# The transpose of a pair's softmax factors: one unit later, and in the bank of the products with V

## The chip, the cores and the metric

One core of a Trainium2 chip. The metric is the device time of one execution in microseconds (us), median over runs. Engines are named as in the profile: PE is TensorE, PEld its weight loads, DVE is VectorE, ACT ScalarE, POOL GpSimd, and SP the SyncE queue that issues all DMAs.

## The reference, cut to what matters

Block-causal attention over 8 batches, 8 heads, 576 positions and 64 columns per head, then a gated convolution layer, then a Fourier mixing layer with a feed-forward net:

```python
scores = scale * np.matmul(q, k.transpose(0, 1, 3, 2))
scores = np.where(mask, scores, -1000000000.0)          # 64-wide blocks, block_i >= block_j
scores = scores - np.max(scores, axis=-1, keepdims=True)
attn = np.exp(scores)
attn = attn / (np.sum(attn, axis=-1, keepdims=True) + 1e-09)
attn_out = np.matmul(attn, v)
...
x = (sigmoid(causal_conv(x)) * (x @ w_val)) @ w_out
u = x + np.real(np.fft.fft(np.fft.fft(x, axis=1), axis=2))
out = u + np.maximum(norm(u) @ w_ch1, 0.0) @ w_ch2
```

What the change touches is the division by the row sums. The kernel multiplies the products with V by the reciprocals of the sums; these are the "softmax factors" of a pair.

## The kernel before, in words

The kernel has two phases. Phase 1 does the attention, the gated layer and the Fourier mixing; phase 2 does the normalization and the feed-forward net, and is not touched by the change.

Phase 1 works on pairs of heads: 32 pairs, four to a batch. A pair has nine units. Units 0 to 7 are a tile of 128 query rows of one of the two heads (two heads by four tiles); unit 8 is the last 64 rows of both. The loop at the end of `phase1` steps through all units n; in each step it writes the scores of unit n (tile `sc`, line 406 and 407, or 165 to 167 for unit 8), takes the row maxima (`mx`, line 438) and the exponentials (`PB`, line 451) of units just before, and transposes the exponentials of unit n - 6 (`pt`, line 506; ACT copies them out, line 512). Between them come pieces of the dense work of the batch before (`psv`, `psx`, `psy`, `pss`).

At the step that is ten units behind, `emit_recip` makes the reciprocals `re` of a pair's row sums on DVE (lines 458 to 465). One step later `emit_factors` transposes them on PE (`rt`, line 474) into a PSUM bank of the pool `ps_pt`, whose two banks also take all transposes `pt` and the last piece `ave` of the products with V. ACT copies the ten rows out (line 479), SP writes them to DRAM (`f_d`, line 480) and reads them back three times (line 483), spread over 64 partitions each, into the tile `XF`, since there they are factors along the free axis. After the ninth unit `emit_av` makes the products with V (`av`, line 535, the single bank of the pool `ps_av`; `ave`, a bank of `ps_pt`). `scaled_x` multiplies them by the factors into `XF` on DVE (lines 549 and 548). From `XF` follow the cast `XH` and the first tap `gate` on ACT (lines 57 and 63), the rest `XL` on POOL and four taps on DVE (line 564).

The scores have three banks (`ps_sc`) in turn. A pair fills eight of them: one each for units 0 and 1, and 2 and 3, one each for units 4 to 7, and two for unit 8. So the first scores of a pair take the bank that unit 7 of the pair before held, and can only be written when its exponentials are done.

The order of the instructions on an engine is not simply that of the code: a scheduler places each instruction by the order of the code and by its own idea of when its inputs are ready. Within an engine the order is then fixed.

`tq` holds the chains of work that wait for a bank of `ps_pt` to be emptied; a `Chain` runs its stages one per step. `load` fetches q and k of a pair two ahead (`qraw`, `kraw`, lines 323 and 325). `spread` writes the queries of the next pair into the tiles `QQ` (lines 377 and 379), `split` into `QD` (line 353); all of these are DMAs of SP too.

Of the kernel before, what the change touches and what calls it, by code (L numbers as in the profile page):

```python
# [8 lines left out]
F32 = mybir.dt.float32  # L9
# [8 lines left out]
def kernel(  # L18
# [14 lines left out]
    B, NP, P, S = q.shape  # L33
    D = 512
# [67 lines left out]
    def phase1():  # L102
        with ExitStack() as c1:
# [6 lines left out]
            ps_pt = c1.enter_context(tc.tile_pool(name="ps_pt", bufs=2, space=bass.MemoryType.PSUM))  # L110
            ps_sc = c1.enter_context(tc.tile_pool(name="ps_sc", bufs=3, space=bass.MemoryType.PSUM))
            ps_av = c1.enter_context(tc.tile_pool(name="ps_av", bufs=1, space=bass.MemoryType.PSUM))
# [71 lines left out]
            def tick(chains):  # L184
                for c in chains:
                    if c.at < len(c.stages):
                        c.run(c.at + 1)
                    if c.at == len(c.stages) and c in live:
                        live.remove(c)
# [128 lines left out]
            def load(p):  # L318
                if p >= NPAIR:
                    return  # L320
                b, hp = divmod(p, NP)
                qraw[p] = raw_p.tile([P, S], F32, tag="raw", name="qraw")
                nc.sync.dma_start(out=qraw[p], in_=q[b, hp])
                kraw[p] = raw_p.tile([P, S], F32, tag="raw", name="kraw")
                nc.sync.dma_start(out=kraw[p], in_=k[b, hp])

            def load_v(p):
                if p >= NPAIR:
                    return
                b, hp = divmod(p, NP)  # L330
                VV[p] = kp.tile([P, 5, P], F32, tag="VV", name="VV")
                nc.sync.dma_start(
                    out=VV[p], in_=v[b, :, hp * P:(hp + 1) * P].rearrange("(t p) c -> p t c", p=P))
# [37 lines left out]
            def spread(p, g):  # L371

                if p >= NPAIR:
                    return
                c = slice(256 * g, 256 * g + 256)
                for h in range(2):
                    nc.sync.dma_start(out=QQ[h][g][rs[h], :, :].bitcast(F32),
                                      in_=QHL[rs[h], 0:1, c].bitcast(F32).to_broadcast([64, 2, 256]))
                    nc.sync.dma_start(out=QQ[h][g][rs[1 - h], 0, :].bitcast(F32), in_=QHL[rs[h], 1, c].bitcast(F32))
# [88 lines left out]
            def emit_factors(p):  # L468

                re = recips.pop(p)  # L470
                if len(tq) > PTB - 1:
                    tq.pop(0).run()
                ps = ps_pt.tile([P, D], F32, tag="pt", name="rt")
                nc.tensor.transpose(ps[0:10, 0:P], re, ident)
                rt = sm.tile([P, P], F32, tag="rt", name="rt", bufs=2)
                to, fd = XFS[p % NXF], f_d[p % 2]

                def out():
                    nc.scalar.copy(out=rt[0:10], in_=ps[0:10, 0:P])
                    nc.sync.dma_start(out=fd, in_=rt[0:10])  # L480
                    row = fd.rearrange("c q -> (c q)").unsqueeze(0)
                    for h, at, n, c in ((0, 0, S, 0), (1, 768, 512, 0), (1, 704, 64, 512)):
                        nc.sync.dma_start(out=to[rs[h], c:c + n], in_=row[:, at:at + n].to_broadcast([64, n]))
                tq.append(Chain(out))

            tq = []
            VY = 3
            PTB = 2
# [26 lines left out]
            fin, recips = {}, {}  # L515

            def emit_av(p):

                if p - 1 in fin:
                    fin[p - 1].run(1)  # L520
                t = ps_av.tile([P, D], F32, tag="av", name="av")
                if len(tq) > PTB - 1:
                    tq.pop(0).run()
                e = ps_pt.tile([P, D], F32, tag="pt", name="ave")
                for to, q0, n, nj in ((t, 0, 256, 2), (t, 256, 256, 4), (e, 512, 64, 5)):
                    for j in range(nj):

                        a = max(q0, P * j) if q0 < 512 else q0
                        w = q0 + n - a
                        for h in range(2):  # L530
                            r = slice(64 * h, 64 * h + 64)
                            src = (PTA[p % 2][:, h, 256 * j:] if q0 == 0 else PTb[:, h, j, a - 256:] if j < 4 else
                                   PTc[:, h, :])
                            o = a % 512
                            nc.tensor.matmul(to[r, o:o + w], VV[p][:, j, r], src[:, 0:w],  # L535
                                             start=(j == 0), stop=(j == nj - 1))
                finish_x(p, t, e)
# [4 lines left out]
            def finish_x(p, t, e):  # L542
                c = p % NP
                xh, xl = xs_of(p // NP)[c]
                XF = XFS[p % NXF]

                def scaled_x():
                    nc.vector.tensor_tensor(out=XF[:, 512:S], in0=e[:, 0:64], in1=XF[:, 512:S], op=ALU.mult)
                    nc.vector.tensor_tensor(out=XF[:, 0:512], in0=t, in1=XF[:, 0:512], op=ALU.mult)
                first = Chain(scaled_x)  # L550
                tq.append(first)

                def out():
                    first.run()

                def hi():
                    copy(1, xh, XF)

                def lo():
                    nc.gpsimd.tensor_tensor(out=xl, in0=XF, in1=xh.bitcast(F32), op=ALU.subtract)  # L560
                    scaled(2, gate[c], XF, cw[:, c, 4:5])

                def tap(s):
                    nc.vector.scalar_tensor_tensor(  # L564
                        out=gate[c][:, s:S], in0=XF[:, 0:S - s], scalar=cw[:, c, 4 - s:5 - s],
                        in1=gate[c][:, s:S], op0=ALU.mult, op1=ALU.add)

                if p - 1 in fin:
                    fin[p - 1].run()
                fin[p] = Chain(out, hi, lo, *[wait] * TS, lambda: tap(1), *[wait] * TS, lambda: tap(2),  # L570
                               *[wait] * TS, lambda: tap(3), *[wait] * TS, lambda: tap(4))
# [266 lines left out]
            def advance(z, n, emit, less=0):  # L838
                while at[z] < NU and at[z] <= n - less - lags[n >= NS][z]:
                    emit(at[z])  # L840
                    at[z] += 1
# [35 lines left out]
            for n in range(NU + LT + LA):  # L877
                if n == N1:
                    now[0] = 0
                p, i = divmod(n, NB)  # L880
                credit += RATE if n > N0 else RATE0
                nst = int(credit)
                credit -= nst
                if n < NU:
                    if i == 6:
                        load(p + 2)
                    if i == 7:
                        load_v(p + 1)
                    if i == 0:
                        split(p + 1)  # L890
                    emit_qk(n)
                    if i in (4, 8):
                        spread(p + 1, i // 8)
                old = list(live)
                step(nst // 2)
                tick(old)
                advance(0, n, emit_max, 1)
                advance(1, n, emit_exp)
                old = list(live)
                if 0 <= n - LT < NU:  # L900
                    emit_t(n - LT)
                advance(0, n, emit_max)
                pr, ir = divmod(n - FR, NB)
                if n >= FR and pr < NPAIR:
                    if ir == 0:
                        emit_recip(pr)
                    if ir == 1:
                        emit_factors(pr)
                m = n - LT - LA
                if 0 <= m < NU:  # L910
                    pm, im = divmod(m, NB)

                    if im == 8:

                        while pm % NP == 0 and gate_done[0] < pm // NP:
                            step()
                        if pm % NP == 0 and pm:
                            folds[4 * (pm // NP) - 2].run(2)
                        while pm % NP == 1 and pm > NP and val_done[0] < pm // NP:
                            step()  # L920
                        emit_av(pm)
                        if pm % NP == NP - 1:
                            pend.append(dense(pm // NP))
                step(nst - nst // 2)
                tick(old)
# [279 lines left out]
```

## Time and profile before

| | |
|---|---|
| median of 3 runs | 1520.55 us (1520.42 to 1522.08) |
| the profiled execution: its time | 1518.6 us |
| the profiled execution: span of its instructions | 1516.8 us |
| mean granted TensorE clock | 0.985 |
| PE busy, share of the span | 1430.2 us, 94% |
| DVE | 831.0 us, 55% |
| ACT | 648.1 us, 43% |
| POOL | 302.6 us, 20% |

Phase 1 ends at about 640 to 700 us. Its first 200 us also fetch and decode the weights; from 200 us to 640 us the same four pairs repeat six times, with the dense work of the batch before between them. From 640 us to 800 us DVE is the busiest engine, after that PE. The busy shares of the whole span are a mean over these stretches, so the change, which lies in phase 1, is read from the rows of 50 to 640 us. In a row, the time in brackets is how long the engine stood idle before the instruction, and after the arrow stands what ended that.

### The profile page before, as it was taken

How to read it: one execution, taken by the hardware profiler on the slowest of the kernel's cores; microseconds unless marked ns; L12 is line 12 of the kernel's file. 1: busy time of each engine (PE TensorE's matmuls, PEld its weight loads, DVE VectorE, ACT ScalarE, POOL GpSimd, SP SyncE). 2: the span in 40 equal slices, each digit the busy share in tenths (PEclk: the TensorE clock that was granted, in tenths of full speed). 3: DMA queues.
4: the chain of work that ended last, by engine and by line, in shares of the span. 5: the costliest groups of instructions: out<-in, count | busy, mean ns of one | idle time of the engine just before them, and what ended most of it. 6: DMA issues, size and time to landing. Idle time of an engine off the chain costs nothing.

```text
span 1516.8 us, 23187 instructions
## 1 busy us (share of the span) xinstructions
PE 1430.2 (94%) x8588; PEld 1207.8 (80%) x8588; DVE 831.0 (55%) x1712; ACT 648.1 (43%) x1642; POOL 302.6 (20%) x244
## 2 busy tenths in 40 slices
PE   5688999999999999998999999999999999999998
PEld 3466788888888888986677888888888888888887
DVE  5668687878787878689995223213223222322212
ACT  5577767676767686734452212112121211212110
POOL 2322232323232323122001111011111100111100
PEclk9699999999999999999999999999999999999999
DMA  7566565656565656133441010010101001010000
GB/s 208 150 158 200 132 176 158 167 138 173 137 176 137 176 132 173 46 135 126 168 140 56 0 56 1 1 55 0 56 0 56 1 10 46 1 56 0 29 0 28
DMA packets 122592, 138.75 MB, mean 91 GB/s; under 512 B 24112, under 2 KB 92016, under 8 KB 122480
## 3 DMA queue, kind: packets, MB, share of 16 engines
q1 hardware_dynamic: 122480, 137.27, 31.5%
q8 instruction: 68, 1.11, 0.3%
q14 instruction: 44, 0.36, 0.1%
HBM read 72.05 MB, written 19.04 MB: 60 GB/s over the span
## 4 chain that ended last, share of the span: by engine, by line
PE 50%; DVE 10%; issue 1%; POOL 0%; ACT 0%; DMA 0%; SPq 0%; DVEq 0%; POOLq 0%
PE o L1097 8%; PE psh L1079 8%; PE psh L1078 8%; PE psh L1077 8%; PE o L1095 8%; PE o L1096 8%; DVE st L74 1%; DVE st L76 1%; DVE st L84 1%; DVE st L72 1%; DVE W1L L989 1%; PE av L535 1%; DVE W2L L989 1%; DVE hl L1083 0%; PE pt L506 0%
## 5 line engine op out<-in xcount | busy, mean ns | idle before, releaser
L1083 DVE SCALAR_TENSOR_TENSOR hl<-psh,hh 128x512 fp32r<-128x512 f32 x144 | 99.4, 690 | 397.2 <-ACT hh L1082 397.1
L1082 ACT ACTIVATE hh<-psh 128x512 fp32r<-128x512 f32 x144 | 85.9, 597 | 510.7 <-PE psh L1079 510.7
L1097 PE MATMUL o<-hl,W2H 128*128 128x512 f32 x576 | 220.7, 394 | 13.2 <-DVE hl L1083 13.1
L1079 PE MATMUL psh<-UTH,W1L 128*128 128x512 f32 x576 | 225.4, 391 | 0.9 <-DVE W1L L989 0.9
L1077 PE MATMUL psh<-UTH,W1H 128*128 128x512 f32 x576 | 224.8, 391 | 0.8 <-ACT UTH L1042 0.8
L1078 PE MATMUL psh<-UTL,W1H 128*128 128x512 f32 x576 | 225.0, 391 | 0.4 <-DVE UTL L1043 0.4
L1095 PE MATMUL o<-hh,W2H 128*128 128x512 f32 x576 | 224.1, 389 | 0.0
L1096 PE MATMUL o<-hh,W2L 128*128 128x512 f32 x576 | 224.0, 389 | 0.0
L451 ACT ACTIVATE PB<-sc,mx 128x128 f32<-128x128 f32 (+4 forms) x320 | 165.6, 522 | 39.6 <-DVE mx L438 21.9
L506 PE MATMUL pt<-ident,PB 128*128 128x128 f32 x800 | 142.7, 284 | 17.7 <-ACT PTb L512 7.4
L1097 PEld LDWEIGHTS o<-hl,W2H 128*128 128x128 f32 x576 | 107.6, 189 | 40.9 <-DVE hl L1083 19.2
L506 PEld LDWEIGHTS pt<-ident,PB 128*128 128x128 f32 x800 | 100.4, 144 | 35.0 <-ACT PTb L512 13.5
L1077 PEld LDWEIGHTS psh<-UTH,W1H 128*128 128x128 f32 x576 | 108.6, 189 | 24.0 <-ACT UTH L1042 1.1
L1079 PEld LDWEIGHTS psh<-UTH,W1L 128*128 128x128 f32 x576 | 108.5, 188 | 24.0 <-DVE W1L L989 1.3
L1078 PEld LDWEIGHTS psh<-UTL,W1H 128*128 128x128 f32 x576 | 108.7, 189 | 23.6 <-DVE UTL L1043 0.9
L1095 PEld LDWEIGHTS o<-hh,W2H 128*128 128x128 f32 x576 | 108.1, 188 | 22.8 <-ACT hh L1082 0.2
L1096 PEld LDWEIGHTS o<-hh,W2L 128*128 128x128 f32 x576 | 108.1, 188 | 22.6
L564 DVE SCALAR_TENSOR_TENSOR gate<-XF,cw,gate 128x575 f32<-128x575 f32 (+3 forms) x128 | 123.5, 965 | 2.1 <-ACT gate L63 1.1
L1106 POOL TENSOR_TENSOR U<-o,U 128x512 f32<-128x512 f32 x32 | 40.3, 1290 | 364.8 <-DVE o L1104 364.8
L438 DVE TENSOR_REDUCE mx<-sc 128x1 f32<-128x384 f32 (+2 forms) x192 | 104.4, 561 | 4.9 <-PE sc L167 2.8
L406 PE MATMUL sc<-K,QQ 128*128 128x256 f32 (+2 forms) x256 | 88.6, 356 | 18.6 <-DMA QQ<-QHL 15.4
L560 POOL TENSOR_TENSOR XL<-XF,XH 128x576 fp32r<-128x576 f32 x32 | 45.6, 1426 | 276.7 <-ACT XH L57 268.9
(191 smaller groups left out, 2879.4 us busy)
## 6 DMA issues: line engine op xcount, KB each, us to landing
K<-KP SPq DMA_DIRECT2D x128, 144.0 KB, 2.6
QQ<-QHL SPq DMA_DIRECT2D x128, 128.0 KB, 3.5
rw<-in_w_ch SPq DMA_DIRECT2D x32, 512.0 KB, 4.2
VV<-in_v SPq DMA_DIRECT2D x32, 320.0 KB, 4.3
qraw<-in_q SPq DMA_DIRECT2D x32, 288.0 KB
kraw<-in_k SPq DMA_DIRECT2D x32, 288.0 KB, 5.9
out<-U SPq DMA_DIRECT2D x36, 256.0 KB, 2.0
QQ<-QHL SPq DMA_DIRECT2D x128, 64.0 KB, 2.0
```

The source lines that it names most:

```text
L406: nc.tensor.matmul(t[:, o:o + w], q[:, 0, m], KK[p][h][:, 0:w], start=True, stop=False)
L438: nc.vector.reduce_max(out=mx[:, j:j + 1], in_=t, axis=AX.X, negate=one)
L451: nc.scalar.activation(out=PB[i][:, k0:k0 + w], in_=t, func=AF.Exp, bias=nm, accum_out=su[:, i + j:i + j + 1])
L506: nc.tensor.transpose(ps[:, j, :], PB[i][:, (j0 + j) * P:(j0 + j + 1) * P], ident)
L564: nc.vector.scalar_tensor_tensor(out=gate[c][:, s:S], in0=XF[:, 0:S - s], scalar=cw[:, c, 4 - s:5 - s], in1=gate[c][:, s:S], op0=ALU.mult, ...
L1077: nc.tensor.matmul(ps, W1H[f][:, c, :], UTH[g][:, c, :], start=(c == 0), stop=False)
L1078: nc.tensor.matmul(ps, W1H[f][:, c, :], UTL[g][:, c, :], start=False, stop=False)
L1079: nc.tensor.matmul(ps, W1L[f][:, c, :], UTH[g][:, c, :], start=False, stop=(c == 3))
L1083: nc.vector.scalar_tensor_tensor(out=l, in0=ps, scalar=0.0, in1=h.bitcast(F32), op0=ALU.max, op1=ALU.subtract)
L1095: nc.tensor.matmul(po[t], W2H[e][:, c], h, start=(e == 0), stop=False)
L1096: nc.tensor.matmul(po[t], W2L[e][:, c], h, start=False, stop=False)
L1097: nc.tensor.matmul(po[t], W2H[e][:, c], l, start=False, stop=(e == NF - 1))
```

## The change

- `emit_factors` runs one unit later (`ir == 2` in place of `ir == 1`).
- The transpose of the factors goes to the bank of `ps_av` in place of a bank of `ps_pt`. As that bank holds the products with V of the pair before, `scaled_x` of the pair before is emitted first, which `emit_av` did until now.
- The copy out of the bank is no entry of `tq` any more; it is kept in `facs` and is run by `emit_av` at the latest, which takes the bank next.

```diff
@@ emit_factors
                 re = recips.pop(p)
-                if len(tq) > PTB - 1:
-                    tq.pop(0).run()
-                ps = ps_pt.tile([P, D], F32, tag="pt", name="rt")
+
+                if p - 1 in fin:
+                    fin[p - 1].run(1)
+                ps = ps_av.tile([P, D], F32, tag="av", name="rt")
                 nc.tensor.transpose(ps[0:10, 0:P], re, ident)
...
-                tq.append(Chain(out))
-
+                facs[p] = Chain(out)
+
+            facs = {}
@@ emit_av
-                if p - 1 in fin:
-                    fin[p - 1].run(1)
+                facs.pop(p).run()
                 t = ps_av.tile([P, D], F32, tag="av", name="av")
@@ the loop over units
-                    if ir == 1:
+                    if ir == 2:
                         emit_factors(pr)
```

The DMA queue of SP around the factors of pair 14 (counted from 0), before. `f_d` is the write to DRAM, `XF` the three reads back, `QQ` and `QD` queries of the next pair, `qraw` and `kraw` the fetches for a later one:

```order
L353 DMA QD0_112<-QHL_111 64x2x64 x2
L480 DMA f_d0_65<-rt_3971 10x128
L379 DMA QQ00_114<-QHL_111 64x256
L377 DMA QQ10_116<-QHL_111 64x2x256
L379 DMA QQ10_116<-QHL_111 64x256
L483 DMA XF0_131<-f_d0_65 64x576
L483 DMA XF0_131<-f_d0_65 64x512
L483 DMA XF0_131<-f_d0_65 64x64
L323 DMA qraw_4052<-in_q 128x576
L325 DMA kraw_4054<-in_k 128x576
```

The same place now:

```order
L353 DMA QD0_112<-QHL_111 64x2x64 x2
L377 DMA QQ00_114<-QHL_111 64x2x256
L379 DMA QQ00_114<-QHL_111 64x256
L377 DMA QQ10_116<-QHL_111 64x2x256
L379 DMA QQ10_116<-QHL_111 64x256
L481 DMA f_d0_65<-rt_3990 10x128
L323 DMA qraw_4052<-in_q 128x576
L325 DMA kraw_4054<-in_k 128x576
L484 DMA XF0_131<-f_d0_65 64x576
L484 DMA XF0_131<-f_d0_65 64x512
L484 DMA XF0_131<-f_d0_65 64x64
```

The write now stands behind four `QQ`, and the reads back stand behind `qraw` and `kraw`.

PE at the same pair, before (`pt` from `PB5` and `PB6` are the transposes of units 5 and 6, `psx` is dense work):

```order
L506 MATMUL pt_3962<-ident_70,PB5_123 128x128 x3
L474 MATMUL rt_3969<-ident_70,re_3932 10x128
L165 MATMUL psx_3950<-GH2_158,we_h_154 128x290
L166 MATMUL psx_3950<-GL2_162,we_h_154 128x290
L167 MATMUL psx_3950<-GH2_158,we_l_155 128x290
L165 MATMUL psx_3950<-GH3_159,we_h_154 128x290
L166 MATMUL psx_3950<-GL3_163,we_h_154 128x290
L167 MATMUL psx_3950<-GH3_159,we_l_155 128x290
L506 MATMUL pt_3991<-ident_70,PB6_124 128x128 x4
```

And now:

```order
L508 MATMUL pt_3962<-ident_70,PB5_123 128x128 x3
L165 MATMUL psx_3950<-GH2_158,we_h_154 128x290
L166 MATMUL psx_3950<-GL2_162,we_h_154 128x290
L167 MATMUL psx_3950<-GH2_158,we_l_155 128x290
L165 MATMUL psx_3950<-GH3_159,we_h_154 128x290
L166 MATMUL psx_3950<-GL3_163,we_h_154 128x290
L167 MATMUL psx_3950<-GH3_159,we_l_155 128x290
L508 MATMUL pt_3983<-ident_70,PB6_124 128x128 x4
L475 MATMUL rt_3988<-ident_70,re_3932 10x128
```

The transpose of the factors moved behind six matmuls and four transposes.

DVE at `scaled_x` of pair 13, before (`GL3` is dense work, `sc_3838` the scores of unit 7 of pair 14):

```order
L549 TENSOR_TENSOR XF1_132<-av_3809,XF1_132 128x512
L625 TENSOR_TENSOR GL3_163<-GF1_153,GH3_159 128x580
L548 TENSOR_TENSOR XF1_132<-ave_3810,XF1_132 128x64
L436 MEMSET sc_3838 64x64
L438 TENSOR_REDUCE mx_3847<-sc_3838 128x1
```

And now:

```order
L626 TENSOR_TENSOR GL3_163<-GF1_153,GH3_159 128x580
L436 MEMSET sc_3838 64x64
L550 TENSOR_TENSOR XF1_132<-av_3809,XF1_132 128x512
L549 TENSOR_TENSOR XF1_132<-ave_3810,XF1_132 128x64
L438 TENSOR_REDUCE mx_3847<-sc_3838 128x1
```

`scaled_x` moved behind the dense subtraction and the memset; its two halves now follow each other.

## Rows read from the trace of the kernel before

**Rows 1.** Busy time by stretch: length, PE, PEld, DVE, ACT, POOL, PEclk, DMA, GB/s
```profile
200.00:640.00 440.00, 421.99 (x3640) 384.40 (x3640) 348.37 (x874) 321.43 (x931) 126.55 (x92) 1.00 0.55 149
```

**Rows 2.** Who PE waited for, 200 to 640 us: total us, times, longest
```profile
PE rt L474 <- DVE re L465: 14.7, 17, 1.5
PE pt L506 <- ACT PTb L512: 3.2, 5, 0.6
```

**Rows 3.** The same for PE's weight loads, 200 to 640 us
```profile
PEld sc L406 <- ACT PB L451: 1.3, 5, 0.3
```

**Rows 4.** Timeline of PE: start, duration; factors of pairs 13, 14, 15
```profile
298.00 0.27 PE L474 MATMUL rt<-ident,re 128*10 128x128 f32 x1 [1.30 <-DVE re L465]
...
316.24 0.27 PE L474 MATMUL rt<-ident,re 128*10 128x128 f32 x1 [1.31 <-DVE re L465]
...
317.15 0.60 PE L506 MATMUL pt<-ident,PB 128*128 128x128 f32 x4
...
334.89 0.27 PE L474 MATMUL rt<-ident,re 128*10 128x128 f32 x1 [0.30 <-DVE re L465]
```

**Rows 5.** Timeline of SP's DMA issues at pair 14
```profile
316.77 1.27 SPq L353 DMA_DIRECT2D QD<-QHL  x2
318.13 0.48 SPq L480 DMA_DIRECT2D f_d<-rt  x1
...
319.88 0.59 SPq L379 DMA_DIRECT2D QQ<-QHL  x1
320.57 1.82 SPq L483 DMA_DIRECT2D XF<-f_d  x3
322.49 0.54 SPq L323 DMA_DIRECT2D qraw<-in_q  x1
323.08 0.42 SPq L325 DMA_DIRECT2D kraw<-in_k  x1
```

**Rows 6.** Line 483, the reads back, 200 to 640 us: issue to landing
```profile
DMA to landing us min/median/max: 2.5/3.0/4.1
```

**Rows 7.** Busy time by stretch behind the issue of kraw at 323.08; GB/s is last
```profile
326.50:327.50 1.00, 1.00 (x9) 0.86 (x7) 0.00 (x0) 0.98 (x2) 0.23 (x1) 1.00 0.15 43
```

**Rows 8.** Timelines of DVE, ACT and PE from scaled_x of pair 14
```profile
325.66 0.69 DVE L549 TENSOR_TENSOR XF<-av,XF 128x512 f32<-128x512 f32 x1 [1.12 <-PE av L535]
326.27 0.21 DVE L548 TENSOR_TENSOR XF<-ave,XF 128x64 f32<-128x64 f32 x1
...
326.52 0.67 ACT L57 CAST XH<-XF 128x576 fp32r<-128x576 f32 x1 [1.79 <-DVE XF L548]
...
328.85 0.69 ACT L451 ACTIVATE PB<-sc,mx 128x512 f32<-128x512 f32 x1
...
330.18 0.28 PE L406 MATMUL sc<-K,QQ 128*128 128x256 f32 x1
```

**Rows 9.** Timelines of SP, DVE, ACT and PE at pair 13
```profile
299.87 0.48 SPq L480 DMA_DIRECT2D f_d<-rt  x1
...
306.77 0.69 DVE L549 TENSOR_TENSOR XF<-av,XF 128x512 f32<-128x512 f32 x1 [0.96 <-PE av L535]
...
308.05 0.22 DVE L548 TENSOR_TENSOR XF<-ave,XF 128x64 f32<-128x64 f32 x1
...
309.56 0.67 ACT L451 ACTIVATE PB<-sc,mx 128x512 f32<-128x512 f32 x1
...
310.54 0.28 PE L406 MATMUL sc<-K,QQ 128*128 128x256 f32 x1
```

**Rows 10.** Who PE waited for, 50 to 110 us
```profile
PE sc L406 <- DMA QQ<-QHL: 3.2, 4, 1.7
PE pt L506 <- ACT rt L479: 2.8, 4, 1.7
```

**Rows 11.** Timelines of PE and DVE, 70 to 72 us
```profile
70.34 0.37 PE L474 MATMUL rt<-ident,re 128*10 128x128 f32 x1
...
71.82 0.69 DVE L549 TENSOR_TENSOR XF<-av,XF 128x512 f32<-128x512 f32 x1 [1.63 <-DMA XF<-f_d]
```

## The prediction

> **What bounds the kernel now.** I read the busy time by stretch first. From 200 to 640 us PE is busy for 422.0 of 440 us at full clock, and no other engine for more than 348.4 [rows 1]. So PE sets the pace there, and only its 18.0 us of idle time can be won. Who PE waited for comes next: the reciprocals `re`, in front of the transpose `rt`, 14.7 us in 17 places, and a transpose `pt` waiting for ACT to empty a bank, 3.2 us [rows 2]. These two are all but 0.1 us of the idle time. The timeline of PE shows where they lie: the factors of pair 13 and 14 wait 1.30 and 1.31 us, those of 15 wait 0.30 [rows 4], and those of pair 12 wait for nothing. This group of four repeats six times from 200 us on. `rt` is a single transpose; it stands in PE's fixed order before its input is there, and everything behind it stands still. The change takes aim at exactly this. The second thing to see is a loop with little slack, read from the timelines behind `scaled_x`: its first half begins at 325.66, then come its second half, the cast `XH`, the first tap, and behind these on ACT the exponentials of unit 7, which end at 328.85 + 0.69 = 329.54. PE writes the first scores of the next pair at 330.18, into the bank that these exponentials free [rows 8]. The slack is 0.64 us. At pair 13 the exponentials end at 309.56 + 0.67 = 310.23 and the scores come at 310.54: 0.31 us [rows 9]. That this edge is real shows in the weight loads of those scores, which already wait for the exponentials in five places, 0.3 us each [rows 3]. Whoever delays `scaled_x` by more than the slack delays PE.
>
> **The change part by part.**
>
> *The wait for `re`.* `rt` moves behind six matmuls and four transposes. These end some 1.25 us after the start of `rt` (317.15 for the start of the transposes, and their 0.60 us overlapping with what follows) [rows 4]. That covers the waits of 1.30 within 0.1 and the shorter ones fully. By itself this gives 1.3 + 1.3 + 0.3 = 2.9 us per group of four, 14.7 in all with the uneven ones at the ends [rows 2].
>
> *The bank.* Without `rt` the pool of two banks gives each a longer rest: the transposes behind `rt` no longer find one of them taken. I count the 3.2 us [rows 2] as won, 0.6 per group, since the bank they now get was emptied before. From below the gain is 0: were ACT late for both banks.
>
> *What the new bank adds.* `rt` must wait until `scaled_x` of the pair before has read it, and `av` until ACT has copied `rt`. At pair 14 `scaled_x` of pair 13 is over at 308.27 [rows 9], and `rt` would start at about 317: 9 us to spare. `av` waits for `rt`'s copy by ACT, but by the order of PE it follows only after the transposes of units 7 and 8 and of the next pair's unit 0, so the cover is about three units, 6 us at the 18.24 / 9 = 2.0 us that a unit takes (298.00 to 316.24 [rows 4]). So from 200 us on I cost both at 0. In the first 110 us that cover is missing; see below.
>
> *The DMAs.* These are what gives back. At pair 14 SP's two `QD` end at 316.77 + 1.27 = 318.04, the write `f_d` goes out at 318.13, and the reads `XF` at 320.57, which is 2.44 us after it, while a queue entry takes 0.6 [rows 5]. Now four `QQ` go ahead of the write: it leaves at 318.04 + 4 x 0.64 = 320.6. `qraw` and `kraw` are issued while it is on its way (1.2 us of the 2.44, so they cost SP nothing). The reads go out at 323.0, the second, which is needed for the first half of `scaled_x`, at 323.6. With the median of 3.0 us to landing [rows 6] it is there at 326.6, against a start of `scaled_x` at 325.66 when it waited for `av` alone. That is 0.95 us later, and 0.64 is slack: PE's next scores come 0.3 us later than before, and the 1.3 us won at `rt` are gone, turned into a wait for the bank of the scores. At pair 13 the write stands behind two `QQ` and `kraw`: 299.87 + 3 x 0.6 = 301.65, the second read at 301.65 + 2.44 + 0.6 = 304.7, there at 307.7, against 306.77 [rows 9]. But the dense subtraction no longer stands between the two halves, so `scaled_x` ends at 307.7 + 0.69 + 0.2 = 308.55, 0.28 behind the old 308.27. Slack is 0.31: about 0. At pair 15 I see the reads land before `av` is done, by the same cover of units between issue and last product; 0.3 is kept. Pair 12's `scaled_x` waits for dense work on DVE and not for its factors.
>
> The landing is the number that I don't know: the reads have not stood behind `qraw` and `kraw` before at that pair. The row's ends are 2.5 and 4.1 [rows 6]. I take 3.0, since the stretch three to four us behind `kraw`'s issue at 323.08 moves only 43 GB/s [rows 5, 7]: what both fetch is nearly through by about 326.4, 3.3 us after that issue. Moved with the queue, `kraw` goes out at 321.7 and is through at 325.0, just when the reads' first bytes come.
>
> Here a rule speaks against the change. The Trainium skill, "DMA: Bandwidth & Descriptors", section "Queues, rings and completion order", says that on each DMA engine the descriptors of one issuing queue are consumed in ring order, so a small urgent read stands behind whatever was issued before it. By its figure of about 2 us of fixed cost (section before it) on top of bytes that begin at 325.0, an estimate from that page would put the reads at 327.5 rather than 326.6, and the time to that of the second rival below. The row of the 43 GB/s agrees that the queue drains first; no run here yet shows the reads behind it.
>
> *The sum from 200 us on.* Per group: pair 12 +0.6, pair 13 0, pair 14 -0.3, pair 15 +0.3, together +0.6 us; six groups give 3.6 us. The bounds come from the landing: at 2.5 pair 13 keeps 0.5 and pair 14 keeps 0.2, 1.6 per group, 9.6 us; at 4.1 they lose 1.1 and 1.4, so -1.6 per group, 9.6 us lost.
>
> *The first 200 us.* Between 50 and 110 us PE waits 3.2 us for `QQ` and 2.8 us for ACT to empty the bank that `rt` used [rows 10]. The second goes, and of the first some 0.6 in each of the four places, as `QQ` now leaves ahead of the write. Against this `scaled_x` of pair 1 starts at 71.82, already late by 1.63 us for its factors, while `rt` of pair 2 starts at 70.34 [rows 11]. It will have to wait until `scaled_x` is over, and that gets later by the same four queue entries, 2.5 us, to about 75, while `rt` itself moves by a unit, 2 us at the steady rate [rows 4] and some 3 here: a wait of 1.5 to 2 us for each of three pairs. Gains of 2.8 + 1.5 and losses of 4 to 6 cancel; I take 0, with 6 us either way.
>
> Phase 2 is untouched, and what stands between 640 and 800 us only shifts. The profiled execution took 1518.6 us; less 3.6 that is 1515.0. The median of the runs is 1520.55, 2 us above the profiled one; less 3.6 it is 1517.0, my forecast.
>
> **The rivals.**
>
> *All the waits simply go.* The reads land before `av` is over, because DMA has room at that time. For it: PE waits for nothing else there [rows 2], and the smallest landing is 2.5 us. Against it: the queue positions, which cost 2.5 us before anything else. It would give 1520.55 - 17.9 = 1502.6 if nothing is given back, and 1511 with the landing at 2.5.
>
> *The factors come later than the slack allows, and PE pays at the first scores of each pair.* This is the slower case. Its place is pairs 13 and 14 of every group; its price is one for one, 12 pairs times what the landing exceeds; the point from which it decides is a landing of 3.3 us, where the losses of pairs 13 and 14 (0.3 + 0.6) equal the 0.9 that the others win. At 4.1 us it gives 1520.55 + 9.6 = 1530. For it: the 5 waits already there [rows 3], and `kraw` ahead in the queue. Against it: that 3.0 is the median even now, with other DMAs ahead.
>
> *The early pairs eat what the later ones win.* `rt` stalls behind `scaled_x` three or four times for 2 us or so, with `QQ` no better: 4 us lost, 3.6 won, 1520.5, no change. For it: the late factors at 71.82 [rows 11]. Against it: the waits that PE has there already, 3.2 and 2.8 us [rows 10], can overlap with the new one.
>
> **How the numbers follow.** About 0.2%, 3 us, is what a measurement of this kernel can tell from no change. The forecast gets 0.40; as it lies 3.5 us below the median, a little over half of that, 0.25, is faster by over 0.2%, and 0.15 is the same. All waits gone: 0.15, faster. Late factors: 0.25, of which 0.22 slower and 0.03 the same. Early pairs: 0.20, of which 0.15 the same and 0.05 slower. That makes faster 0.40, same 0.33, slower 0.27. The forecast's own range is 1513 to 1520. For 8 in 10 it reaches to 1508, half way into the first rival, and to 1528, near the end of the second.
>
> **What would show it.** Right, if: no wait of PE for `re` is left from 200 us on beyond 2 us; `scaled_x` waits for the DMA of its factors at pairs 13 and 14 of each group (before, for `av`), by some 1 us; and a new wait for ACT's exponentials stands before the first scores, near 1.3 us at pair 14 and at pair 13. Wrong, if `scaled_x` still waits for `av` (first rival), if the new wait is over 1.5 us (second), or if PE stands before `rt` for the bank. The order of SP decides nothing if the reads land early all the same; that would be the step to fail first.

## The result: 11 us slower, and the profile after

| | before | after |
|---|---|---|
| median | 1521.32 us (4 runs) | 1532.22 us (4 runs, 1530.08 to 1536.14) |
| span of the profiled execution | 1516.8 us | 1528.3 us |
| ratio, with its 95% interval | | 1.0072 [1.0049, 1.0096] |

The forecast was 1517.0, its range ended at 1528, and faster was held likelier than slower. The time lies above all of it, a little beyond what the second rival gave (1530).

Where the 11.5 us of span went can be read from one landmark of PE, the last products with V (`ave`) of a pair. For pair 8 and for pair 28, before and after; behind the colon durations, then start of the first and of the last:

```profile
L535 PE MATMUL ave<-PTb,VV x16: 219/222/222, 209.2 to 209.6; 128*64 128x64 f32 x16
...
L535 PE MATMUL ave<-PTb,VV x16: 219/222/222, 595.9 to 596.3; 128*64 128x64 f32 x16
```

```profile
L536 PE MATMUL ave<-PTb,VV x16: 219/222/222, 212.7 to 213.1; 128*64 128x64 f32 x16
...
L536 PE MATMUL ave<-PTb,VV x16: 219/222/222, 604.7 to 605.1; 128*64 128x64 f32 x16
```

Pair 8 is 3.5 us late, pair 28 is 8.8 us late (8.81 less 3.45, both unrounded): 3.5 us were lost in the first 200 us, 5.4 in the five groups of four that follow. The last 2.7 come behind them, between 660 and 820 us.

PE's waits from 200 to 640 us, after (us, times, longest), which answer to [rows 2]:

```profile
PE rt L475 <- DVE re L465: 6.7, 11, 1.6
PE pt L508 <- ACT PTb L514: 3.1, 5, 0.6
PE sc L406 <- ACT PB L451: 3.1, 4, 1.2
PE pss L165 <- DVE XA L755: 1.8, 3, 0.7
```

The wait for `re` fell by 8.0 us and not by 14.7, the wait for PTb's copy stayed, and two new waits stand there. PE's idle time alone does not show the loss. Over the same work, from the products of pair 8 to those of pair 28, PE does 3189 matmuls in both kernels (columns as in [rows 1], before and after):

```profile
209.22:595.86 386.64, 369.76 (x3189) 336.36 (x3187) 304.36 (x762) 282.94 (x821) 112.05 (x81) 1.00 0.58 157
...
212.67:604.68 392.01, 376.82 (x3189) 335.93 (x3187) 312.76 (x763) 279.88 (x822) 110.76 (x81) 1.00 0.58 155
```

The stretch is 5.4 us longer, but PE's idle time in it (length less busy time) fell from 16.9 to 15.2 us, and its busy time rose by 7.1. Some of the waiting stands at the weight loads. Those of the scores had 1.3 us in 5 places [rows 3], those of `pt` 6.4 us in 10:

```profile
PEld pt L508 <- ACT PTb L514: 12.0, 26, 1.1
...
PEld sc L406 <- ACT PB L451: 7.2, 18, 1.4
```

(The loads of `rt` go the other way, from 17.8 us to 9.3, so the loads alone are no measure of the loss.) And DVE, which in the kernel before waited for `av` at `scaled_x`, now waits for the factors:

```profile
DVE XF L550 <- DMA XF<-f_d: 19.5, 8, 3.3
```

### The profile page after: what moved, and what is told of

The parts are those of the page before. It is cut to its first block, busy times and chain, and to the rows that moved or that the text cites. A ratio compares the mean times of both kernels' runs of the same rounds, so it can differ in the third digit from the quotient of the medians.

```text
span 1528.3 us, 23136 instructions
## 1 busy us (share of the span) xinstructions
PE 1442.8 (94%) x8588; PEld 1213.2 (79%) x8588; DVE 839.1 (55%) x1712; ACT 644.2 (42%) x1642; POOL 301.1 (20%) x244
## 4 chain that ended last, share of the span: by engine, by line
PE 69%; DVE 15%; DMA 5%; ACT 4%; issue 4%; POOL 2%; SPq 2%; DVEq 0%; ACTq 0%; POOLq 0%
PE o L1098 8%; PE psh L1078 8%; PE psh L1080 8%; PE psh L1079 8%; PE o L1096 8%; PE o L1097 8%; PE av L536 5%; PE pt L508 3%; DMA QQ<-QHL 2%; PE sc L406 2%; DVE gate L565 2%; PE sc L407 2%; ACT PB L451 2%; POOL XA L771 1%; PE psv L165 1%
## 5 line engine op out<-in xcount | busy, mean ns | idle before, releaser
L508 PE MATMUL pt<-ident,PB 128*128 128x128 f32 x800 | 145.8, 285 | 23.6 <-ACT PTb L514 14.8
L565 DVE SCALAR_TENSOR_TENSOR gate<-XF,cw,gate 128x575 f32<-128x575 f32 (+3 forms) x128 | 132.4, 1035 | 18.1 <-ACT gate L63 16.9
L406 PE MATMUL sc<-K,QQ 128*128 128x256 f32 (+2 forms) x256 | 90.1, 363 | 18.1 <-DMA QQ<-QHL 14.7
L514 ACT COPY PTb<-pt 128x512 f32<-128x512 f32 (+1 forms) x160 | 86.2, 540 | 23.2 <-PE pt L508 21.8
```

Source lines behind the costliest of these rows:

```text
L406: nc.tensor.matmul(t[:, o:o + w], q[:, 0, m], KK[p][h][:, 0:w], start=True, stop=False)
L508: nc.tensor.transpose(ps[:, j, :], PB[i][:, (j0 + j) * P:(j0 + j + 1) * P], ident)
L565: nc.vector.scalar_tensor_tensor(out=gate[c][:, s:S], in0=XF[:, 0:S - s], scalar=cw[:, c, 4 - s:5 - s], in1=gate[c][:, s:S], op0=ALU.mult, ...
```

## The experiments

Each was timed in five rounds beside the kernel before; the numbers in brackets are the 95% intervals of the ratio. "Offset" is the lateness of a pair's `ave` against the kernel before, read from one execution of each kernel. e9 and e12 treat the first seven pairs as the changed kernel does, and at pair 8 they stand at 5.3 and 3.1 where it stands at 3.5: an offset is good to about 2 us.

### Delay or bank

**e1_delay_only**: the kernel before, one unit later.

```diff
-                    if ir == 1:
+                    if ir == 2:
```

> The transpose of the factors comes one unit later, but stays in a bank of ps_pt, as in the kernel before. The DMA queue of SP then has the order of the changed kernel. Theory of the queue (the factors arrive late, because write and reads stand behind four QQ, qraw and kraw): the 5.4 us that the changed kernel loses between the products of pairs 8 and 28 stay, 4 to 7 us; with less lost in the first 200 us the time is 1526 to 1531. Rival, the bank (the transpose waits for scaled_x of the pair before and then holds up the products): with the old bank nothing is lost from 200 us on, the wait for re goes, and the time is 1515 to 1521.

Measured: 1537.67 us, ratio 1.0104 [1.0087, 1.012]; offset 8.0 at pair 8, 20.3 at pair 28. Slower still than the change as a whole, and above both ranges. The delay is what costs, and the bank of the change takes some of it back (5.5 us here, though the two intervals touch). With the old bank the transposes stand in each other's way:

```profile
PE pt L506 <- ACT PTb L512: 7.1, 11, 1.1
PE sc L406 <- ACT PB L451: 5.5, 6, 1.3
PE rt L474 <- ACT PTb L512: 4.1, 5, 0.9
```

**e2_bank_only**: the changed kernel at the old unit.

```diff
-                    if ir == 2:
+                    if ir == 1:
```

> The transpose goes to the bank of ps_av, but at its old unit (ir == 1); SP's order is that of the kernel before. Theory of the queue: from pair 8 to pair 28 no loss, and the wait for re (14.7 us) stays; -3 to +1 us there; in the first 200 us the transpose waits for scaled_x of the pair before, 0 to 4 us lost; 1518 to 1525. Rival, the bank: the loss of the changed kernel stays or grows, 1529 to 1535.

With the bank go, here too, the earlier `scaled_x` of the pair before and the copy outside `tq`; "the bank" below means all three.

Measured: 1517.98 us, 0.9977 [0.9968, 0.9986]; offset -2.5 at pair 8, -3.4 at pair 28. The bank alone makes the kernel a little faster, in the first 200 us too, where 0 to 4 us were to be lost. The rival that blamed it is refuted. But the gain isn't where I had put it; the wait for PTb's copy is still 3.2 us in 5 places:

```profile
PE rt L475 <- DVE re L465: 14.2, 16, 1.5
PE pt L508 <- ACT PTb L514: 3.2, 5, 0.6
```

**e3_late_dma**: the kernel before; only write and reads go to SP a unit later.

```diff
                     nc.scalar.copy(out=rt[0:10], in_=ps[0:10, 0:P])
+
+                def send():
                     nc.sync.dma_start(out=fd, in_=rt[0:10])
...
                 tq.append(Chain(out))
+                Chain(wait, wait, send)
```

> The kernel before, with transpose and copy where they were; only the write and the reads of the factors are handed to SP one unit later, behind the four QQ, and the reads behind qraw and kraw. Theory of the queue: scaled_x starts late at the third pair of each four and a wait for the exponentials stands before the next pair's first scores, 0.5 to 1.5 us there, with some less at the fourth pair: 2 to 8 us from 200 us on, 1523 to 1531 in all, though transpose and bank are as before. Rival, the bank: no change, 1519 to 1523.

Measured: 1529.48 us, 1.0055 [1.0042, 1.0067]; offset 0.5 at pair 8, 9.2 at pair 28. Transpose, copy and bank are those of before, and so is DVE's order around the reciprocals; 7.7 us are lost by the place of four DMAs in a queue, since DVE now waits for the factors. PE pays in more places than the one expected. Beside the first scores, dense products (`psv`) wait for DVE, and the transpose of the next factors waits for a copy by ACT:

```profile
DVE XF L552 <- DMA XF<-f_d: 16.5, 7, 3.8
...
PE rt L474 <- DVE re L465: 13.8, 15, 1.3
PE psv L165 <- DVE gv L605: 3.3, 2, 2.9
...
PE rt L474 <- ACT XA L660: 3.2, 3, 1.2
PE sc L406 <- ACT PB L451: 1.3, 3, 0.8
```

### The first 200 us apart

**e4_early_old** (pairs 0 to 6 old, the others new) and **e12_late_old** (the other way round):

```diff
-                    if ir == 2:
+                    if ir == (1 if pr < 7 else 2):      # e12: pr >= 7
```

(the bank goes with it).

> The changed kernel, but pairs 0 to 6 have the old unit and the old bank. It shows what the first 200 us cost by themselves. In the changed kernel the products of pair 8 end 3.45 us later than before. If that is the change's doing there (the transpose waits for scaled_x and holds up the products), the time is 3 to 4 us less than that of the changed kernel, 1528 to 1529.5. Rival (the offset at pair 8 is made up anyway where DVE is the bound, 640 to 800 us): the time stays at 1531 to 1533.

> Only pairs 0 to 6 have the new unit and bank, all later pairs the old ones: the first 200 us of the change by themselves. If what the changed kernel lost by pair 8 (3.45 us) is a real cost, 1523 to 1526. If it is made up by waits that fall later, 1519 to 1522.

Measured: e4 1531.31 us, 1.0067 [1.005, 1.0084], offset 0.0 at pair 8 and 8.6 at pair 28; e12 1524.93 us, 1.003 [1.0018, 1.0041], offset 3.1 at pair 8 and 4.3 at pair 28. The early pairs alone cost 3.9 us (1524.93 - 1521.02), the later ones alone 9.5 (1531.31 - 1521.77). Both are clear of the noise. Together they make 10.9 and not 13.4, but with intervals of 2.7 to 6.2 us (e12), 7.6 to 12.8 (e4) and 7.5 to 14.6 (the change) it is not shown whether they add. e4's time lies in its rival's range, though not by the rival's way: nothing had to be made up after 640 us, as the later pairs had lost 8.6 us by pair 28 in this execution, in place of 5.4.

### Late factors, taken away

**e5_no_wait**: the reads go to a spare tile, `scaled_x` multiplies by a constant tile.

```diff
-                        nc.sync.dma_start(out=to[rs[h], c:c + n], in_=row[:, at:at + n].to_broadcast([64, n]))
+                        nc.sync.dma_start(out=dump[p][rs[h], c:c + n], in_=row[:, at:at + n].to_broadcast([64, n]))
...
-                    nc.vector.tensor_tensor(out=XF[:, 512:S], in0=e[:, 0:64], in1=XF[:, 512:S], op=ALU.mult)
+                    nc.vector.tensor_tensor(out=XF[:, 512:S], in0=e[:, 0:64], in1=ident[:, 0:64], op=ALU.mult)
```

(and the other 512 columns likewise). The spare tile lies in DRAM, and the kernel leaves out the division.

> The changed kernel with the same transposes, copies, writes and queue entries, but the three reads back go to a spare DRAM tile and scaled_x multiplies by a constant tile: the division by the row sums is left out, and nothing waits for a factor. Theory of the queue: late factors are all that the delay costs, so from pair 8 to pair 28 no loss is left, the part of the wait for re that the change removed (8 us) and the bank's gain show as such, and the time is 1508 to 1518. Rival (the changed order on DVE and ACT costs by itself: QHL ahead of the reciprocals, scaled_x behind dense work, more work after the copy): the loss stays for the larger part, 1525 to 1533.

Measured: 1508.03 us, 0.9917 [0.9905, 0.9929]; offset -1.7 at pair 8, -11.1 at pair 28. With the full delay, the new bank and every queue entry, but nothing that waits for a factor, the kernel is 12.8 us faster than before. The waits for the exponentials and for `XA` on `pss` are gone, and so is nearly all of the wait for `re`:

```profile
PE rt L475 <- DVE re L465: 0.2, 1, 0.2
```

DVE's order differs here as well: as in the kernel before, the reciprocals come ahead of `QHL` (queries of a later pair), while in the changed kernel they stand behind it at the third pairs. So 12.8 is an upper end of what timely factors give by themselves; e6 takes the two apart.

**e6_factors_first**: copy and DMAs are emitted ahead of the four `QQ`.

```diff
                     if i in (4, 8):
+                        for c in facs.values():
+                            c.run()
                         spread(p + 1, i // 8)
```

> The changed kernel, but the copy and the DMAs of the factors are emitted ahead of the four QQ of the same step. By SP's order the write then leaves ahead of one or two QQ at pairs 12 to 15 of each four; the reads still stand behind qraw and kraw at pairs 14 and 15. So the factors come about 0.65 us earlier at pairs 14 and 15, more at 13. Theory of the queue: the loss from pair 8 to pair 28 falls from 5.4 us to 1 to 3 us, 1525 to 1530. Rival (the changed order on DVE): no change, 1531 to 1533.

Measured: 1517.47 us, 0.9974 [0.9962, 0.9985]; offset -1.6 at pair 8, -2.0 at pair 28. Faster than both ranges: 5.0 us came back by pair 8, and 5.8 between pairs 8 and 28. The 5.8 are not the factors' doing. `qraw` and `kraw` still precede the reads at the third pairs, DVE waits for the factors nearly as long as in the changed kernel (19.5 us there), and PE's new waits stay:

```profile
DVE XF L550 <- DMA XF<-f_d: 17.3, 7, 3.8
...
PE sc L406 <- ACT PB L451: 4.0, 5, 1.3
...
PE pss L165 <- DVE XA L755: 2.1, 3, 1.1
```

What is gone is the wait for `re`: the reciprocals are ahead of `QHL` again, and no row for `re` is left. So the rival's cause, DVE's order, is at work as well. The steady loss of the change has two parts, the late factors and DVE's new order, and without the second alone the steady stretch comes out even.

**e8_pool_queue**: write and reads on POOL's queue.

```diff
-                    nc.sync.dma_start(out=fd, in_=rt[0:10])
+                    nc.gpsimd.dma_start(out=fd, in_=rt[0:10])
```

(and the three reads likewise).

> The changed kernel, but the write and the reads of the factors are issued by POOL's queue in place of SP's, so they don't stand behind QQ, qraw and kraw. Theory of the queue: the factors land some 2 us earlier at pairs 14 and 15, the loss of 5.4 us goes and some of the wait for re is won, 1515 to 1524; POOL stands still while a write is on its way, which costs something if the subtractions XL come late. Rival (the changed order on DVE): 1529 to 1536. If POOL's own order makes the factors later still: over 1536, which tells nothing between the two.

Measured: 1538.15 us, 1.0111 [1.0094, 1.0128]. The third case: POOL issues the reads only when the write has landed and its own subtractions are done, so the factors are later than on SP, with 28.5 us of DVE waiting for them (19.5 in the changed kernel). It says nothing between the two theories, as its expectation allowed.

**e9_load_pool**: only `qraw` and `kraw` leave SP's queue.

```diff
-                nc.sync.dma_start(out=qraw[p], in_=q[b, hp])
+                (nc.gpsimd if p > 9 else nc.sync).dma_start(out=qraw[p], in_=q[b, hp])
```

(and `kraw` likewise).

> The changed kernel, but from pair 10 on the fetches qraw and kraw are issued by POOL's queue in place of SP's. The write and the reads of the factors keep their place behind four QQ; only nothing of qraw and kraw is ahead of the reads on their queue. In the changed kernel the factors are there 3.6 to 4.7 us (mean 4.1) after the issue of the second read at the third pair of each four, and 3.0 to 3.2 us at the second pair, where kraw is farther ahead. Theory of the ring (the reads stand behind the bytes of qraw and kraw on their queue): 3.0 to 3.3 us at the third pair too, and 3 to 6 us of the loss from pair 8 on goes, 1525 to 1530. Rival (DMA engines are shared whatever the queue): 3.8 us or more, and 1530 to 1534.

Measured: 1524.20 us, 1.002 [1.0009, 1.0031]; offset 5.3 at pair 8, 6.7 at pair 28, so 1.4 us lost where the changed kernel loses 5.4. POOL, SP and DVE at pair 14 in e9, then SP and DVE in the changed kernel:

```profile
319.40 0.56 POOL L323 DMA_DIRECT2D qraw<-in_q  x1 [0.41 <-POOL KL L359]
...
322.59 0.56 POOL L325 DMA_DIRECT2D kraw<-in_k  x1 [1.77 <-DVE sc L429]
...
326.30 0.46 SPq L481 DMA_DIRECT2D f_d<-rt  x1
327.90 1.77 SPq L484 DMA_DIRECT2D XF<-f_d  x3
...
331.56 0.69 DVE L550 TENSOR_TENSOR XF<-av,XF 128x512 f32<-128x512 f32 x1 [1.25 <-DMA XF<-f_d]
```

```profile
324.77 0.47 SPq L481 DMA_DIRECT2D f_d<-rt  x1
325.34 0.35 SPq L323 DMA_DIRECT2D qraw<-in_q  x1
325.74 0.41 SPq L325 DMA_DIRECT2D kraw<-in_k  x1
326.37 1.76 SPq L484 DMA_DIRECT2D XF<-f_d  x3
...
330.77 0.69 DVE L550 TENSOR_TENSOR XF<-av,XF 128x512 f32<-128x512 f32 x1 [2.80 <-DMA XF<-f_d]
```

The reads leave 1.6 us behind the write in both. From their issue to `scaled_x` it is 331.56 - 327.90 = 3.66 us without `qraw` and `kraw` ahead in the queue, and 330.77 - 326.37 = 4.40 with them. Over the third pairs of the groups that waited for DMA: 3.66 to 3.79 (3 pairs) against 4.16 to 5.19, mean 4.67 (5 pairs). From the second read it is 3.1 to 3.2 us in e9, in the range of the ring theory. So the two fetches directly ahead cost the reads about 1 us. That the order of the ring does it is not shown, since e9 moved the fetches in time as well as to another queue: POOL issues them 8.5 and 5.3 us ahead of the reads (1.0 and 0.6 in the changed kernel), and the second, 3.1 us on its way, has landed 2.2 us before the reads leave. Shared DMA engines, the rival, would then cost nothing either. A run with the fetches on another queue at the same moment would tell the two apart, and there is none. Some of the 4 us won are DVE's (its order moved a little too, and the wait for `re` is 1.2 us), so the offset is no measure of the fetches alone; the 3.7 against 4.7 is.

### Half of the delay

**e7_half_unit**: bank as in the change; the transpose at the end of its old step.

```diff
-                    if ir == 2:
-                        emit_factors(pr)
...
                 step(nst - nst // 2)
+                if n >= FR and pr < NPAIR and ir == 1:
+                    emit_factors(pr)
                 tick(old)
```

> The transpose goes to the bank of ps_av as in the changed kernel, but stands at the end of its old step, behind the dense products of that step and ahead of the transposes of the next unit: half of the delay. SP's order at pairs 13 and 14 is that of the kernel before, at pair 12 the write stands behind QD, at pair 15 the reads stand behind qraw alone. Theory of the queue: the cover of six products takes some 0.9 us of each wait for re, at 12 of the 17 places, and the factors are not later: 1505 to 1514, faster than with the bank alone (1518). Rival (any later transpose makes the chain behind it late): 1518 to 1525.

**e10_half_unit_old_bank**: the same, in a bank of `ps_pt`.

```diff
-                ps = ps_av.tile([P, D], F32, tag="av", name="rt")
+                if len(tq) > PTB - 1:
+                    tq.pop(0).run()
+                ps = ps_pt.tile([P, D], F32, tag="pt", name="rt")
```

> The transpose at the end of its old step as in e7_half_unit, but in a bank of ps_pt as in the kernel before. If delay and bank add up, the bank is worth here what it was at the old unit (3 us from e2_bank_only): 1510 to 1515. If the old bank hurts more when the transpose stands close to the next unit's transposes, which then find one of two banks taken (as it did with the full delay, 1537.7 against 1532.2), 1515 to 1521.

**e11_next_step**: as e7, behind the first dense work of the next step.

```diff
                 step(nst // 2)
+                pr, ir = divmod(n - FR, NB)
+                if n >= FR and pr < NPAIR and ir == 2:
+                    emit_factors(pr)
+                    old.append(facs[pr])
                 tick(old)
```

> As e7_half_unit, but the transpose stands behind the first dense work of the next step in place of the end of its own, and the copy is run in that same step. In SP's order the factors stay where e7_half_unit has them. It differs only where dense products psv stand: one group of three further back there. The wait for re left in e7_half_unit (6.0 us) falls by 0 to 2 us: 1506 to 1511. Rival (the copy, now right behind the transpose, makes ACT late): 1511 to 1517.

Measured: e7 1509.54 us, 0.9923 [0.9908, 0.9939], offset -3.0 at pair 8 and -11.3 at pair 28; e10 1515.32 us, 0.9963 [0.995, 0.9975]; e11 1510.75 us, 0.9931 [0.9918, 0.9944]. e7 and e11 are 10 to 11 us faster than the kernel before, and not told apart from each other, though e11's wait for `re` is 3.2 us. Both come near e5, in which nothing waits for factors. e7's SP at pair 14 has the write and the reads where the kernel before has them [rows 5], ahead of `qraw`:

```profile
313.12 0.48 SPq L481 DMA_DIRECT2D f_d<-rt  x1
...
315.55 1.82 SPq L484 DMA_DIRECT2D XF<-f_d  x3
317.48 0.54 SPq L323 DMA_DIRECT2D qraw<-in_q  x1
```

The cover of six products is enough for most of the wait for `re` (6.0 us left of 14.7), and no unit of the queue is lost. e10, at the border of its two ranges, says what the bank is for here: with the old one the time is 5.8 us longer, and the wait for PTb's copy, 3.1 us in 5 places in e7, is

```profile
PE pt L510 <- ACT PTb L516: 8.0, 16, 0.7
```

At the old unit the bank was worth 3.8. The intervals (e7 9.3 to 14.0 us faster, e10 3.8 to 7.6) don't tell 5.8 from 3.8, so whether bank and delay add up is open.

## Why the prediction was wrong

The second rival is what happened from 200 us on, in more places than it had; the forecast put it at 0.25. Beside it stand a loss in the first 200 us and DVE's new order, which no rival had. Of some 15 us between forecast and result, about 9 lie in the steady stretch (3.6 to be won, 5.4 lost), 3.5 before it and 2.7 behind.

The steady stretch can be read by steps from one pair's products to the next, as the change of a step against the kernel before, in us, mean of the five groups from pair 8 on; negative is faster. The forecast's terms are put where they act: the wait of `rt` of a pair in the step to its products, its late `scaled_x` in the step behind.

| step | forecast | changed | e6 | e7 | e5 |
|---|---|---|---|---|---|
| first pair of a group to the second | -1.3 | -0.54 | -0.63 | -0.70 | -0.27 |
| second to third | 0 | -0.01 | -1.29 | -0.85 | -1.18 |
| third to fourth | 1.3 | 1.15 | 1.21 | -0.17 | -0.44 |
| fourth to the next group's first | -0.6 | 0.48 | 0.62 | 0.06 | 0.00 |

In the second row the forecast's 0 was 1.3 won at `rt` of the third pair and 1.3 given back by the late factors of the second. In the changed kernel `scaled_x` waits under 0.1 us for the factors of the second pairs, so nothing is given back there, and `rt` of the third pair still waits 0.8; e6, where it doesn't, wins the 1.3. So both terms were wrong, and the 0 was luck. In the third row, too, the size is luck: the factors were later than forecast, but as nothing had been won at `rt`, there was less to give back. What made the sum wrong stands in the first row and the last: the wins at the second pairs were smaller (the waits for `re` there were 0.59 to 1.51 us, not 1.3 each time, and the first group lost 0.55), the bank's 0.6 was not won, and the factors of the fourth pairs, counted as in time, cost 0.5. Step by step:

- *The wait for `re`*: "That covers the waits of 1.30 within 0.1 and the shorter ones fully". Right for pairs 12 and 13 of each group: `rt` of pair 13 starts at 302.46 with no wait, and PE's time from the products of pair 12 to those of 13 fell from 19.52 to 18.47 us. Wrong for pair 14. There DVE's order had moved too: `QHL`, 0.75 us long, now stands ahead of the reciprocals, and `rt` still waits 0.78 or 0.79 us at four of the five third pairs (1.05 at pair 10):

```profile
319.91 0.75 DVE L348 SCALAR_TENSOR_TENSOR QHL<-qraw,QHL 128x576 fp32r<-128x576 f32 x1
320.58 0.23 DVE L464 RECIPROCAL re<-su 128x4 f32<-128x4 f32 x2
...
320.92 0.28 PE L475 MATMUL rt<-ident,re 128*10 128x128 f32 x1 [0.79 <-DVE re L465]
```

  The prediction took the cover against a `re` that stands still; it had looked at DVE's order around `scaled_x` only. In e5, e6, e7 and e11 the reciprocals come first again.

- *The DMAs*: the queue was right, the landing failed: "I take 3.0". PE's products of pair 14 begin 3.43 us later than before:

```profile
323.18 0.65 PE L535 MATMUL av<-PTa,VV 128*64 128x256 f32 x4
```

```profile
326.61 0.65 PE L536 MATMUL av<-PTa,VV 128*64 128x256 f32 x4
```

  Less that, the write left at 324.77 - 3.43 = 321.34 (forecast 320.6), the reads at 322.94 (forecast 323.0), and `scaled_x` started at 327.34 (forecast 326.6). The reads' 322.94 is luck: the write left 0.7 us late, and from write to reads it was 1.6 us in place of 2.44. From the second read to `scaled_x` it was 3.6 to 4.7 us at the five third pairs, mean 4.1, which was the forecast's far end. At the second pairs from 13 on, where `kraw` is 3 us ahead, it was 3.0 to 3.2. The forecast took the median of landings that had no `qraw` and `kraw` directly ahead. The prediction gave the rival 0.25 on the ground that "3.0 is the median even now, with other DMAs ahead", and set against it the 43 GB/s of [rows 7], which say that the fetches were through, and nothing of the order behind them.

  The estimate from the Trainium skill ("DMA: Bandwidth & Descriptors", section "Queues, rings and completion order": each DMA engine takes a queue's descriptors in ring order) was 327.5; its 2 us of fixed cost are given, in the section before, for DMAs that GpSimd issues, and these are SP's. The measured 327.34 agrees with it, but e9 shows only that the fetches directly ahead cost 1 us, not that the ring does it.

- *The slack*: 327.34 is 1.68 us behind 325.66; less the slack of 0.64, 1.0 us is due at the next first scores. At pair 14 that was the price: PE's period from its products to those of pair 15 grew by 0.93. (The prediction's slack at pair 13 has two slips, 0.67 for the row's 0.69 and 308.55 for 308.59: the slack is 0.29 and the delay 0.32. The step behind pair 13 shows no loss from it.) At pair 18 one sees the chain whole, in DVE, ACT and PE:

```profile
408.56 0.69 DVE L550 TENSOR_TENSOR XF<-av,XF 128x512 f32<-128x512 f32 x1 [3.33 <-DMA XF<-f_d]
...
409.42 0.67 ACT L57 CAST XH<-XF 128x576 fp32r<-128x576 f32 x1 [4.00 <-DVE XF L549]
...
411.11 0.70 ACT L451 ACTIVATE PB<-sc,mx 128x512 f32<-128x512 f32 x1
...
411.95 0.38 PE L406 MATMUL sc<-K,QQ 128*128 128x256 f32 x1 [0.91 <-ACT PB L451]
```

  This loop and its slack at pair 14 were right; of the two places forecast, the third pairs pay and the second don't.

- *What stands behind the waiting instruction*: missed. `scaled_x` holds DVE for up to 3.33 us, and everything queued behind it is late, not only the exponentials. Of pair 15 the prediction saw "the reads land before `av` is done". At pair 15 itself they did, but at pairs 19, 23 and 27 `scaled_x` waited 2.1 to 2.2 us for them. At pair 19 the factors come at 427.64, 1.0 us behind the products, the dense addition `XA` follows late, and PE's `pss` waits for it:

```profile
427.64 0.69 DVE L550 TENSOR_TENSOR XF<-av,XF 128x512 f32<-128x512 f32 x1 [2.22 <-DMA XF<-f_d]
...
431.82 0.44 DVE L755 TENSOR_TENSOR XA<-pss,XA 128x290 f32<-128x290 f32 x1
...
432.32 0.29 PE L165 MATMUL pss<-dft,YCH 128*2 128x290 f32 x1 [0.69 <-DVE XA L755]
```

- *The bank*: "I count the 3.2 us [rows 2] as won". Nothing of it was: 3.1 after, 3.2 in e2. Those five waits stand right before the products of each group's first pair, some 7 us behind its `rt` (277.63 at pair 12 in the kernel before), so `rt` was not what held the bank:

```profile
284.56 0.33 PE L506 MATMUL pt<-ident,PB 128*128 128x128 f32 x1 [0.64 <-ACT PTb L512]
284.82 0.44 PE L535 MATMUL av<-PTa,VV 128*64 128x256 f32 x2
```

  The bank's worth is elsewhere, as e2 and e10 show.

- *The first 200 us*: "I take 0, with 6 us either way". It was 3.5 in the trace, 3.9 by e12, inside the bounds. The forecast expected `rt` to wait for the bank, and no such wait stands there. From 50 to 110 us, after, against [rows 10], `av` waits for the copy of `rt`, once, and the transposes for PTb's copy:

```profile
PE pt L508 <- ACT PTb L514: 7.4, 9, 2.0
PE av L536 <- ACT rt L480: 2.9, 1, 2.9
...
PE sc L406 <- DMA QQ<-QHL: 1.4, 1, 1.4
```

  The gains named there came (no wait for `rt`'s copy at `pt` is left, `QQ` fell from 3.2 to 1.4). What made the loss is open. e2 and e7, ahead by 2.5 and 3.0 us at pair 8, have the same two waits there (1.6 and 7.8 us in e2, 1.7 and 6.2 in e7). The granted clock of the first 50 us is lower in the changed kernel (0.80, against 0.87 before), but in e2 it is 0.81.

- *The end of phase 1*, which "only shifts": not quite. The offset grows from 8.7 at pair 30 to 11.1 soon behind 800 us, and in two stretches of it the granted clock (third number from the right) is under that of the kernel before, which has 1.00 in both:

```profile
680.00:700.00 20.00, 18.72 (x124) 17.82 (x124) 19.24 (x36) 9.87 (x22) 3.85 (x4) 0.91 0.33 99
...
800.00:820.00 20.00, 17.12 (x67) 13.71 (x68) 17.77 (x31) 8.35 (x15) 0.44 (x1) 0.91 0.07 21
```

  The kernel before has its lower clock from 700 to 740 us (0.92 and 0.91; the changed one 1.00 and 0.84). e4, e6, e7, e9, e11 and e12 show shifts of 1.2 to 2.3 us behind pair 30 as well, the other six runs under 0.7. Whether they follow from the change was not tried and stays open.

## What to carry to other kernels

A wait that is taken from the busiest engine by moving an instruction later moves its successors too; follow all of them through every queue, and price a DMA by what stands directly ahead of it in the new order, not by its landings in the old one. Where an engine is made to wait, list what is queued behind the waiting instruction, since all of it is late. Look at the order of every engine that feeds the moved instruction too: here DVE's order moved with it, and e6, which has the old order again, loses nothing in the steady stretch. And ask how much delay the stall needs: here half a unit covered most of it (1509.5 us) and a whole unit cost more than it covered (1532.2).

## What the hardware showed that was not expected

The reads of the factors were in use 1 us later when two fetches had left the same queue directly ahead of them than when the fetches had landed before (4.16 to 5.19 us from issue to use, against 3.66 to 3.79). Whether the order of the queue or the shared DMA engines make the 1 us, no run shows.

And time that PE loses need not show as idle time: over the same 3189 matmuls the stretch grew by 5.4 us, while PE's idle time fell by 1.7 and its busy time rose by 7.1. Late weight loads are a likely reason (those of the scores waited 7.2 us, 1.3 before), but no run shows it.
